# Matmuls on zeros ahead of the first inputs, and the last row's normalising factor by square root and reciprocal

## The chip, the core and the metric

The kernel runs on one NeuronCore of a Trainium2 chip. The core has five engines, each with its own instruction queue that is worked off in order: TensorE (PE, matrix products into PSUM), VectorE (DVE), ScalarE (ACT), GpSimd (POOL) and SyncE (SP, which here issues DMAs only). The metric is device time in microseconds; of three runs of the kernel before the median is 1186.96 us, with 1186.71 and 1188.21 at the ends.

## What is computed

The input is a sequence of 2048 positions with 576 channels. Four layers follow one another, each added to its input: Fourier mixing (A), a gated long convolution (B), A again, B again.

```python
def _A_ref(x, dft_seq_re, dft_seq_im, dft_hid_re, dft_hid_im):
    a = jnp.einsum("bsd,ed->bse", x, dft_hid_re)
    b = jnp.einsum("bsd,ed->bse", x, dft_hid_im)
    return jnp.einsum("ts,bse->bte", dft_seq_re, a) - jnp.einsum("ts,bse->bte", dft_seq_im, b)
...
x = A_x
x = x + _A_ref(_layernorm(x, axis=-1), A_dft_seq_re, A_dft_seq_im, A_dft_hid_re, A_dft_hid_im)
x = x + _B_ref(_layernorm(x, axis=-1), B_k, B_v, B_shift_k, B_ssm_k, B_ssm_D)
x = x + _A_ref(_layernorm(x, axis=-1), A_dft_seq_re, A_dft_seq_im, A_dft_hid_re, A_dft_hid_im)
x = x + _B_ref(_layernorm(x, axis=-1), B_k, B_v, B_shift_k, B_ssm_k, B_ssm_D)
```

`_layernorm` subtracts the mean of a row's 576 channels and divides by the square root of their variance plus 1e-5. The convolution branch of B depends on the weights and on B_k and B_v alone, so its result is computed once; in both B layers the normalised row is then multiplied by it, element by element.

## The kernel before

**Tiles.** The 2048 positions lie as 16 row blocks (J = 16) of 128 partitions by 576 channels. The sequence transform of layer A is done first: for each of four blocks of 512 output positions, for the cosine and for the sine matrix, the 16 row blocks are summed up in PSUM. One such pair of a row block and a 128x512 tile of the transform matrix is called a step here, and step k of the first sixteen uses row block Xk and matrix tile ck. [...] A step multiplies hi by hi, hi by lo and lo by hi for four groups of 128 channels (12 matmuls into the accumulators `acc4`, tiles `s`) and, for the last 64 channels, does two more (tile `rm`): 14 matmuls of 512 columns (lines 318 to 332).

**What feeds a step.** Row block Xk is loaded from HBM (line 683), its statistics are taken on DVE (lines 181 to 183: two `bn_stats`, one `bn_aggr`, the variance plus 1e-5), GpSimd raises that to the power -1/2 (line 184), DVE makes the bias (line 190) and ACT normalises the row (line 191). From row block 8 on (`ASTAT`) ACT takes the sums instead (lines 649 and 651, with lines 650, 652 and 675 on DVE and the power on GpSimd, line 653; line 676 normalises). Then ACT writes the hi part (line 195) and DVE the lo part (lines 197 and 198). Matrix tile ck is loaded to a raw buffer (lines 168 and 216); ACT writes its hi part and DVE its lo part (lines 98 and 99 for the tile `mats`). There are three buffers for split matrix tiles, so the hi part of c(k+3) has to wait until step k has been multiplied.

**Beside it.** In the first steps runs the branch that prepares the convolution: its inputs are loaded (lines 366, 374, 418), combined on DVE (lines 393 and 398, 128x1152 each), split (lines 98 and 99, tile `f1r`) and multiplied in groups of six matmuls of 288 columns (tile `bf`, line 448), which ACT copies out of PSUM (line 451) and stores (line 452).

**Order.** The code is traced by generators: `layer` yields after pieces of a step, and the driver behind line 746 runs pieces of the branch between them. A planner at compile time then lays out each engine's instructions from what it knows of dependencies and costs; `tc.issue_after` (lines 101 to 106, `behind`) ties an instruction behind another one on its engine. So an engine's order in the trace need not be the order of the code.

**The end.** The last row blocks go through `hidden` (lines 276 to 289: 27 matmuls for each half of a row, added on DVE at line 287) and `done1`, where `gated` takes the statistics of the row (`norm_stats`), forms (row - mean) times the branch (line 665) and then multiplies by the factor and adds the row (line 668). For the last row block, j = 15, line 668 is done in two halves, and each half is sent to HBM at once (line 739, the first half from ACT's queue, the second from SP's).

**What the change touches.** The small tile `flts` (line 156) with -1/2 in its first column (lines 157 and 174); one ACT copy into its second column, which makes the ACT load its function table early (line 175); `gated` (line 656); and the driver between lines 750 and 751, where the first row block's load has been issued and no other work has been traced.

Of the kernel before, what the change touches and what calls it, by code (L numbers as in the profile page):

```python
# [10 lines left out]
F32 = mybir.dt.float32  # L11
FR = mybir.dt.float32r
AF = mybir.ActivationFunctionType
OP = mybir.AluOpType

P = 128
# [3 lines left out]
J = S // P  # L20
TB = 4
NT = 512
HD = D // 2
NC = 4
REM = D - NC * P
EPS = 1e-5
ASTAT = 8
XLEAD = 3
EARLY = 6
ROWS = (0, 1, 2, 3, 4, 5, 6, 7, 8, 9)  # L30
K_FIRST = 4
# [34 lines left out]
def fnet_h3_kernel(ctx: ExitStack, tc: tile.TileContext, x, c_mat, w_re, w_im, k_pad, v, shift_k,  # L66
                   ssm_k, ssm_d, f1c, i2c, midc, out):
    nc = tc.nc
# [5 lines left out]
    def mm(ps, lhsT, rhs, first, last, more=False):  # L74
        return nc.tensor.matmul(ps, lhsT, rhs, start=first, stop=last, skip_group_check=more).ins  # L75
# [10 lines left out]
    acc4 = [psp.tile([P, NT], F32, tag=f"s{i}", name=f"s{i}") for i in range(4)]  # L86
# [25 lines left out]
    def flat(words, dt, name):  # L112
        return sb.tile([P, words], dt, tag=name, name=name)
# [15 lines left out]
    ring = {}  # L129

    def lay(t, at, *sizes):

        for name, words, n in sizes:
            ring.setdefault(name, Ring()).tiles.extend(t[:, at + i * words:at + (i + 1) * words] for i in range(n))
            at += n * words
        assert at <= t.shape[1], (at, t.shape, sizes)
        return at
# [9 lines left out]
    xs = mats[:, :X_END].rearrange("p (j n) -> p j n", j=J)  # L147
# [6 lines left out]
    um = []  # L154

    flts = flat(FLT, F32, "flts")
    mhalf = flts[:, :1]
    lay(flts, 8, ("stat", STAT, 4))
    lay(flts, RT_AT, ("rt", NT, 1))
    lay(mats, X_END, ("cs", WIDE, 3))  # L160
# [5 lines left out]
    def load_after(dst, src):  # L166
        with tc.issue_after(anchor[-1]):
            return nc.sync.dma_start(dst, src).ins
# [3 lines left out]
            nc.gpsimd.dma_start(dst, src)  # L172

    nc.vector.memset(mhalf, -0.5)
    nc.scalar.activation(flts[:, 1:2], mhalf, AF.Copy)

    def norm_stats(src):
        m = ring["stat"]()
        st, mv, ve, rs = m[:, :12].rearrange("p (a c) -> p a c", a=2), m[:, 12:14], m[:, 14:15], m[:, 15:16]
        for i in range(2):  # L180
            nc.vector.bn_stats(st[:, i, :], src[:, i * HD:(i + 1) * HD])
        nc.vector.bn_aggr(mv, st)
        nc.vector.tensor_scalar(ve, mv[:, 1:2], EPS, None, op0=OP.add)  # L183
        pows.append(nc.gpsimd.tensor_tensor(rs, ve, mhalf, OP.pow).ins)  # L184
        return mv, rs, m[:, 16:17]
# [27 lines left out]
    def load_c(step):  # L213
        g, tb, k = step
        raw = ring["craw"]()
        anchor.append(load_after(raw, c_mat[g, tb, k]) if anchor else nc.sync.dma_start(raw, c_mat[g, tb, k]).ins)
        c = ring["cs"]()
        t = c[:, :NT], c[:, NT:]
        with behind(*stored):
            halved[:] = split(t[0], t[1], raw)  # L220
        CT[step] = t
# [3 lines left out]
    def load_w():  # L225
        lay(flts, SC_AT + CRAW * NT + 4 * D, ("wl", D, 3))
        wg = region_a(FR, "w").rearrange("p (k n) -> p k n", k=9)
        for ch in (8, *range(8)):
            w = two(wg[:, ch])
            raw = ring["wl"]()  # L230
            if ch < 8:
                nc.sync.dma_start(raw, (w_re if ch < 4 else w_im)[(ch % 4) * P:(ch % 4 + 1) * P, :])
            else:
                nc.sync.dma_start(raw[:REM], w_re[NC * P:, :])
                nc.sync.dma_start(raw[REM:], w_im[NC * P:, :])
            for lo, hi, sg in ((0, P, 1 if ch < 4 else -1),) if ch < 8 else ((0, REM, 1), (REM, P, -1)):
                if sg > 0:
                    split(w[lo:hi, 0, :], w[lo:hi, 1, :], raw[lo:hi])
                else:
                    nc.scalar.activation(w[lo:hi, 0, :], raw[lo:hi], AF.Copy, scale=-1.0)  # L240
                    nc.vector.scalar_tensor_tensor(w[lo:hi, 1, :], raw[lo:hi], -1.0,  # L241
                                                   w[lo:hi, 0, :].bitcast(F32), op0=OP.mult,
                                                   op1=OP.subtract)
            W[ch] = w
            yield
        for ch in range(9):
            load_after(w_d[ch], wg[:, ch].bitcast(F32))
            yield
# [42 lines left out]
    def finish(pending, pieces):  # L291
        while pending and pieces:
            if not isinstance(pending[0], types.GeneratorType):
                pending[0] = hidden(*pending[0])
            if next(pending[0], 0) == 0:
                pending.pop(0)
            else:
                pieces -= 1

    def layer(get_x, xres, done, pending, blocks=TB):  # L300
        steps = [(g, tb, k) for tb in range(blocks) for g in range(2) for k in range(J)]
        for n, (g, tb, k) in enumerate(steps):
# [3 lines left out]
            if n + 2 < len(steps):  # L306
                load_c(steps[n + 2])
            for i in range(XLEAD + 1 if blocks == TB else 1):
                if n + i < J:
# [336 lines left out]
    def sums(src, junk):  # L646
        m = ring["stat"]()
        sm, sv, rs, nb = (m[:, i:i + 1] for i in range(4))
        nc.scalar.activation(junk, src, AF.Copy, accum_out=sm)
        nc.vector.tensor_scalar(sm, sm, -1.0 / D, None, op0=OP.mult)  # L650
        nc.scalar.activation(junk, src, AF.Square, bias=sm, accum_out=sv)
        nc.vector.tensor_scalar(sv, sv, 1.0 / D, EPS, op0=OP.mult, op1=OP.add)
        pows.append(nc.gpsimd.tensor_tensor(rs, sv, mhalf, OP.pow).ins)
        return sm, rs, nb

    def gated(xa, q, j, junk=None, last=None):
        load_after(q, yb_d[j])
        if junk is None:
            mv, rs, _ = norm_stats(xa)
            mean, op = mv[:, 0:1], OP.subtract  # L660
        else:
            mean, rs, _ = sums(xa, junk)
            op = OP.add
        yield
        nc.vector.scalar_tensor_tensor(q, xa, mean, q, op0=op, op1=OP.mult)
        for i in range(2 if last else 1):
            cs = slice(i * HD, (i + 1) * HD) if last else slice(None)
            nc.vector.scalar_tensor_tensor(q[:, cs], q[:, cs], rs, xa[:, cs], op0=OP.mult, op1=OP.add)
            if last:
                last(i, cs)  # L670

# [8 lines left out]
    def load_x(j):  # L680
        if j < J:
            XL[j] = ring["x"]()
            nc.sync.dma_start(XL[j], x[:, j, :])
# [7 lines left out]
    def get_x0(j):  # L691
        if X[j] is None:
            if j > 0:
                load_x(j + 2)
            stats0(j)
            if j > 0:
                with behind(*stored):
                    stats0(j + 1)
            src, ln = LN[j]
            with behind(*rounded[-1:]):  # L700
                next(ln, 0)
            X[j] = to_x(src, j)
# [4 lines left out]
    def make_x1(j):  # L707
        xa, q = ring["xa"](), ring["yb"]()
        load_after(xa, xa_d[j])
        for _ in gated(xa, q, j, ring["xj"]() if j % 2 and j >= EARLY else None):  # L710
            yield
        for _ in normed_x(q, xa, ring["xj"]()):
            to_store.append((xb_d[j], q))
            yield
        to_store.append((y_d[j // 2][:, j % 2, :], xa))
        X[j] = to_x(xa, j)
        ready.add(j)
# [3 lines left out]
    def advance(j=None):  # L721
        while to_store:
            load_after(*to_store.pop(0))
        with behind(*halved, *added, *evac):
            for row in list(making):
                if next(row, 0) == 0:
                    making.remove(row)
            if j is not None:
                making.append(make_x1(j))
                next(making[-1])  # L730
# [4 lines left out]
    def done1(j, xa):  # L735
        q = ring["yb"]()

        def store(i, cs):
            (nc.scalar if i == 0 else nc.sync).dma_start(out[:, j, cs], q[:, cs])

        for _ in gated(xa, q, j, last=store if j == J - 1 else None):
            pass
        if j < J - 1:
            nc.sync.dma_start(out[:, j, :], q)

    pending = []
    lay(flts, SC_AT, ("craw", NT, CRAW))
    br = branch()
    wl = load_w()
    load_x(0)  # L750
    next(br)
    get_x0(0)
    with tc.issue_after(biased[0]):
# [18 lines left out]
    for n, whole in layer(get_x0, lambda j: x[:, j, :], done0, pending):  # L772
# [30 lines left out]
        m = n - PREP  # L803
# [9 lines left out]
        if 0 <= m and n < HOLD:  # L813
            advance(m // 2 if m % 2 == 0 and m < 2 * EARLY else None)
    T, R, t7 = {}, {}, []
# [126 lines left out]
    cs, done = {}, []  # L942
# [68 lines left out]
    for n, whole in layer(get_x1, lambda j: xb_d[j], done1, pending, 1):  # L1011
# [4 lines left out]
        if n == 0:  # L1016
            for name, at in (("xa", 0), ("yb", 4 * D)):
# [3 lines left out]
                lay(gate, at, (name, D, 4))  # L1021
        advance(EARLY + ROWS.index(n) if n in ROWS else None)
        finish(pending, 1)
# [131 lines left out]
```

## Time and profile before

| what | value |
|---|---|
| median of three runs | 1186.96 us |
| the profiled execution's own time | 1186.46 us |
| its span, first to last instruction | 1184.5 us |
| time outside the span | 1.96 us |
| PE busy / weight loads busy | 1165.9 / 988.1 us |
| DVE / ACT / POOL busy | 868.8 / 650.6 / 75.0 us |

A row of the timeline gives the start of a group of equal instructions in us from the start of the span, how long the group lasts, the engine, the line of the kernel, the operation, what it writes and reads, the size and how many there are; in brackets stands the idle time of the engine before it and what ended that. An engine name with a q (SPq, ACTq) is the engine's own queue work, such as issuing a DMA. [...]

### The profile page before, as it was taken

Reading aid. Unit: us, or ns where it says so; the run is one execution under the profiler, and the core shown is the slowest. Engines: PE = TensorE matmul, PEld = TensorE weight load, DVE = VectorE, ACT = ScalarE, POOL = GpSimd, SP = SyncE. Lnnn points to the kernel's source line nnn. Section 1 sums busy time; section 2 is a strip of 40 time slices with the busy share of each in tenths; the row PEclk is TensorE's granted clock in tenths of the full one; section 3 lists DMA queues with packets and bytes.
Section 4 is the critical chain, followed back from the end, with each engine's and each line's share of the span. In section 5 each row is a group of like instructions: output and inputs, shape, how many; then the busy total and the mean of one; then the engine's idle time right before and its main releaser. Section 6 shows DMA issues by size and latency. Waiting matters only on the chain.

```text
span 1184.5 us, 18056 instructions
## 1 busy us (share of the span) xinstructions
PE 1165.9 (98%) x6184; PEld 988.1 (83%) x6184; DVE 868.8 (73%) x1562; ACT 650.6 (55%) x1279; POOL 75.0 (6%) x116
## 2 busy tenths in 40 slices
PE   7999999999999999999999999999999999999997
PEld 5776767888888888888888898888888888789997
DVE  7899983688877778787757765865776777775764
ACT  7865655578766668766645666534434445440200
POOL 2210000000000000001101111000000000001111
PEclk9999999999999999999999999999999999999999
DMA  9869898546666656648966776763762777894621
GB/s 341 297 194 313 268 294 267 177 148 182 213 198 201 198 169 201 193 139 250 267 191 218 244 251 232 246 239 88 251 240 72 244 271 255 270 318 157 212 84 41
DMA packets 147454, 255.65 MB, mean 216 GB/s; under 512 B 16161, under 2 KB 56353, under 8 KB 147362
## 3 DMA queue, kind: packets, MB, share of 16 engines
q1 hardware_dynamic: 111890, 210.17, 55.5%
q10 hardware_dynamic: 28560, 37.91, 9.1%
q0 software_dynamic: 6912, 6.43, 2.5%
q8 instruction: 48, 0.79, 0.3%
q14 instruction: 44, 0.36, 0.1%
HBM read 187.80 MB, written 66.65 MB: 215 GB/s over the span
## 4 chain that ended last, share of the span: by engine, by line
PE 77%; ACT 2%; DMA 1%; DVE 1%; issue 0%; ACTq 0%; POOLq 0%; DVEq 0%
PE s L75 43%; PE bk L75 30%; PE rm L75 4%; ACT flts L512 1%; ACT mid L512 1%; DMA t<-ud 1%; DMA flts<-in_c_mat 0%; ACT mats L98 0%; DVE mid L518 0%; DVE flts L532 0%; DVE flts L531 0%; DVE t L99 0%; ACT u L98 0%; POOLq L1151 0%; ACTq L548 0%
## 5 line engine op out<-in xcount | busy, mean ns | idle before, releaser
L75 PE MATMUL s<-mats 128*128 128x512 f32 x2088 | 542.3, 395 | 1.1 <-ACT mats L195 1.0
L75 PEld LDWEIGHTS s<-mats 128*128 128x128 f32 x2088 | 381.0, 188 | 82.2 <-issue 10.6
L99 DVE TENSOR_TENSOR mats<-flts,mats 128x512 fp32r<-128x512 f32 x206 | 140.7, 687 | 52.2 <-ACT mats L98 51.0
L98 ACT ACTIVATE mats<-flts 128x512 fp32r<-128x512 f32 x206 | 128.3, 627 | 82.8 <-PE bk L75 29.6
L75 PE MATMUL bk<-mid 128*128 128x288 f32 x704 | 126.4, 300 | 1.4 <-DVE flts L287 0.6
L75 PEld LDWEIGHTS bk<-mid 128*128 128x128 f32 x704 | 108.5, 188 | 22.0 <-ACT flts L512 5.0
L512 ACT ACTIVATE flts<-bk 128x288 f32<-128x288 f32 (+1 forms) x192 | 76.5, 405 | 90.2 <-PE bk L75 76.5
L75 PE MATMUL bk<-w,u 128*128 128x288 f32 x864 | 120.9, 295 | 0.4 <-DVE w L241 0.4
L75 PEld LDWEIGHTS bk<-w,u 128*128 128x128 f32 x864 | 117.5, 188 | 3.7 <-ACT flts L512 0.9
L518 DVE TENSOR_TENSOR mid<-flts,mid 128x576 fp32r<-128x576 f32 (+1 forms) x149 | 93.4, 627 | 19.0 <-ACT mid L512 16.3
L75 PE MATMUL rm<-mats 128*128 128x512 f32 x304 | 94.8, 391 | 0.2 <-ACT flts L512 0.2
L512 ACT ACTIVATE mid<-flts 128x576 fp32r<-128x576 f32 (+1 forms) x148 | 80.5, 576 | 9.6 <-DVE flts L533 5.1
L287 DVE TENSOR_TENSOR flts<-flts,bk 128x288 f32<-128x288 f32 x48 | 21.8, 453 | 66.8 <-PE bk L75 64.3
L75 PE MATMUL bk<-mats 128*128 128x288 f32 (+1 forms) x376 | 67.8, 317 | 0.0
L451 ACT ACTIVATE flts<-bf 128x384 f32<-128x384 f32 (+1 forms) x104 | 43.1, 463 | 44.9 <-PE bf L75 44.8
L75 PEld LDWEIGHTS rm<-mats 128*128 128x128 f32 x304 | 57.1, 188 | 12.8 <-ACT flts L512 0.6
L75 PE MATMUL s<-t,mats 128*128 128x512 f32 x264 | 65.4, 390 | 0.6 <-DVE t L99 0.3
L184 POOL TENSOR_TENSOR flts<-flts 128x1 f32<-128x1 f32 x35 | 28.7, 820 | 521.9 <-DVE flts L183 521.8
L75 PE MATMUL bk<-mats,t 128*128 128x288 f32 (+1 forms) x368 | 59.3, 303 | 0.0
L75 PEld LDWEIGHTS s<-t,mats 128*128 128x128 f32 x264 | 49.4, 188 | 11.7 <-DVE t L99 0.8
L512 ACT ACTIVATE flts<-flts 64x288 f32<-64x288 f32 x128 | 56.6, 442 | 4.5
L75 PEld LDWEIGHTS bk<-mats 128*128 128x128 f32 x376 | 55.6, 188 | 3.4
(146 smaller groups left out, 1495.3 us busy)
## 6 DMA issues: line engine op xcount, KB each, us to landing
flts<-in_c_mat SPq DMA_DIRECT2D x148, 256.0 KB, 3.4
ph<-in_c_mat SPq DMA_DIRECT2D x54, 512.0 KB, 4.3
flts<-in_c_mat SPq DMA_DIRECT2D x30, 512.0 KB, 5.1
flts<-td SPq DMA_DIRECT2D x53, 288.0 KB, 3.0
td<-flts ACTq DMA_DIRECT2D x36, 384.0 KB, 4.5
vd<-flts ACTq DMA_DIRECT2D x64, 144.0 KB, 2.5
flts<-vd SPq DMA_DIRECT2D x32, 288.0 KB, 4.0
ud<-ph ACTq DMA_DIRECT2D x12, 512.0 KB, 6.6
```

What stands on the lines that cost most here:

```text
L75: return nc.tensor.matmul(ps, lhsT, rhs, start=first, stop=last, skip_group_check=more).ins
L98: a = nc.scalar.activation(h, src, AF.Copy).ins
L99: return a, nc.vector.tensor_tensor(l, src, h.bitcast(F32), OP.subtract).ins
L184: pows.append(nc.gpsimd.tensor_tensor(rs, ve, mhalf, OP.pow).ins)
L287: added[:] = [nc.vector.tensor_tensor(r[:, cs], r[:, cs], ps[:, :HD], OP.add).ins]
L451: stored[:] = [nc.scalar.activation(so[:, i, :], ps[i], AF.Copy).ins]
L512: last_act.append(nc.scalar.activation(*args, **kw).ins)
L518: nc.vector.tensor_tensor(l, src, h.bitcast(F32), OP.subtract)
```

## The change

At the start, DVE writes zeros into the first 512 columns of the place where row block 15 will be put later, and TensorE multiplies these zeros by themselves 14 times, 128x128 by 128x512, into the accumulator `acc4[3]`. Nothing reads the product: the first real matmul into `acc4[3]` starts its sum anew.

For the last row block alone, `gated` leaves out the addition of 1e-5 on DVE and the power on GpSimd. ACT takes the square root of the variance plus 1e-5 (given as the bias, from a third column of `flts`), and DVE takes the reciprocal after line 665. The early ACT instruction that makes it load its table is a square root now instead of a copy. All other rows keep the power on GpSimd.

```diff
+WARM = 14
...
-    mhalf = flts[:, :1]
+    mhalf, eps = flts[:, :1], flts[:, 2:3]
...
     nc.vector.memset(mhalf, -0.5)
-    nc.scalar.activation(flts[:, 1:2], mhalf, AF.Copy)
+    nc.vector.memset(eps, EPS)
+    nc.scalar.activation(flts[:, 1:2], eps, AF.Sqrt)
...
     def gated(xa, q, j, junk=None, last=None):
         load_after(q, yb_d[j])
-        if junk is None:
+        if last:
+            m = ring["stat"]()
+            st, mean, var = m[:, :12].rearrange("p (a c) -> p a c", a=2), m[:, 12:13], m[:, 13:14]
+            for i in range(2):
+                nc.vector.bn_stats(st[:, i, :], xa[:, i * HD:(i + 1) * HD])
+            nc.vector.bn_aggr(m[:, 12:14], st)
+            rs, op = m[:, 14:15], OP.subtract
+            nc.scalar.activation(var, var, AF.Sqrt, bias=eps)
+        elif junk is None:
             mv, rs, _ = norm_stats(xa)
             mean, op = mv[:, 0:1], OP.subtract
...
         nc.vector.scalar_tensor_tensor(q, xa, mean, q, op0=op, op1=OP.mult)
+        if last:
+            nc.vector.reciprocal(rs, var)
         for i in range(2 if last else 1):
...
+    def warm():
+        t = xs[:, J - 1, :NT]
+        nc.vector.memset(t.bitcast(F32), 0.0)
+        for i in range(WARM):
+            mm(acc4[3], t[:, :P], t, i == 0, i == WARM - 1)
+
...
     load_x(0)
+    warm()
     next(br)
     get_x0(0)
```

More of the change, by code (lines that the diff above doesn't have):

```diff
@@ L665, in gated @@
         nc.vector.scalar_tensor_tensor(q, xa, mean, q, op0=op, op1=OP.mult)
+        if last:
+            nc.vector.reciprocal(rs, var)
         for i in range(2 if last else 1):
             cs = slice(i * HD, (i + 1) * HD) if last else slice(None)
-            nc.vector.scalar_tensor_tensor(q[:, cs], q[:, cs], rs, xa[:, cs], op0=OP.mult, op1=OP.add)
+            nc.vector.scalar_tensor_tensor(q[:, cs], q[:, cs], rs, xa[:, cs],
+                                           op0=OP.mult, op1=OP.add)
             if last:
```

## The prediction

> **What bounds the kernel now.** I read the page's busy times first, then PE's waits over the whole span, then the timeline of its two ends, where the change lies.
>
> ```profile
> PE 1165.9 (98%) x6184; PEld 988.1 (83%) x6184; DVE 868.8 (73%) x1562; ACT 650.6 (55%) x1279; POOL 75.0 (6%) x116
> ```
> ```profile
> PE bf L75 <- DVE f1r L99: 6.6, 1, 6.6
> PE s L75 <- ACT mats L195: 1.0, 2, 0.8
> ```
> PE is busy for 98% of the span. Of the 18.6 us in which it is not, 6.6 are the wait for the first inputs, and the next longest wait is 0.8 us. So what can be won lies in the wait at the start, in the rate just behind it, and after the last matmul.
>
> ```profile
> 6.61 1.09 PE L75 MATMUL bf<-f1r 64*128 64x288 f32 x6 [6.61 <-DVE f1r L99]
> 7.92 1.73 PE L75 MATMUL s<-mats 128*128 128x512 f32 x2 [0.22 <-ACT mats L195]
> 9.66 1.09 PE L75 MATMUL bf<-f1r 64*128 64x288 f32 x6
> 10.68 4.53 PE L75 MATMUL s<-mats 128*128 128x512 f32 x10
> 15.04 0.63 PE L75 MATMUL rm<-mats 128*128 128x512 f32 x2
> 15.51 2.88 PE L75 MATMUL s<-mats 128*128 128x512 f32 x12
> 18.23 0.62 PE L75 MATMUL rm<-mats 128*128 128x512 f32 x2
> 18.68 2.88 PE L75 MATMUL s<-mats 128*128 128x512 f32 x12
> ...
> 21.95 0.67 PE L75 MATMUL bf<-f1r 64*128 64x288 f32 x6
> 22.54 3.05 PE L75 MATMUL s<-mats 128*128 128x512 f32 x12
> ```
> Step 0 begins at 7.92 and step 1 at 15.51. Ten matmuls start between 10.68 and 15.04, 0.436 us each; in step 1 twelve start between 15.51 and 18.23, 0.227 each. TensorE thus runs at half its later rate until about 14.9, 8.3 us after its first matmul. At 0.227 the ten would take 2.3 us instead of 4.4. The product groups `bf` show the same: 1.09 us early, 0.67 later.
>
> **Part 1, the zeros.** They remove nothing; they add one DVE memset and 14 matmuls ahead of PE's first work.
>
> ```profile
> 0.81 0.06 DVE L174 MEMSET flts<- 128x1 f32 x1 [0.81 <-PEq L1147]
> 3.66 0.82 DVE L181 BATCH_NORM_STATS2 flts<-early 128x6 f32<-128x288 f32 x2 [2.79 <-DMA early<-in_x]
> ```
> A memset of 128x512 is not in the trace. The 128x1 one bounds it below (0.06 us), a DVE subtraction of that size (0.68, the row of line 198 below) above. It is one pass over one operand, so I take the upper end. Both small memsets and this one lie in DVE's 2.79 us of idling, so they cost nothing; behind them waits the first `bn_stats`, which would be late only if they lasted until 3.66. PE can then start at 1.0 to 1.7. At 0.427 to 0.436 the 14 matmuls take 6.0 to 6.1 us and end by 7.8 at the latest, against the 6.61 at which real work is ready. That delays the first `bf` group by up to 1.2 us, to 7.8 to 8.9. Behind it stands step 0's first matmul (7.92), and its second needs the lo part of c0, written at 8.12 to 8.79. The ACT copy of that group's result starts at 8.91 (below). So the delay costs 0.1 us or nothing, more so as the rate should have doubled by then: PE took 8.3 us with gaps from its first matmul until the doubling, and 8.3 us after 1.5 is 9.8, without gaps sooner.
>
> With the rate doubled before 9.66, the second `bf` group (held until 9.60 by the ACT copy of the first) lets step 0 go on at 9.66 + 0.59 = 10.25 (0.59 is 22.54 - 21.95). Its remaining 12 matmuls at 0.227, with 0.1 for the switch between shapes, end at 13.1. Before, the next step began at 15.51: **2.4 us**. What has to be ready next is X1:
>
> ```profile
> 8.12 0.67 DVE L99 TENSOR_TENSOR mats<-flts,mats 128x512 fp32r<-128x512 f32 x1
> 8.91 0.69 ACT L451 ACTIVATE flts<-bf 128x288 f32<-128x288 f32 x2
> 13.55 0.67 ACT L195 ACTIVATE mats<-early 128x576 fp32r<-128x576 f32 x1
> 15.09 0.68 DVE L198 TENSOR_TENSOR mats<-early,mats 128x512 fp32r<-128x512 f32 x1
> ```
> Its hi part is there at 14.22, its lo part at 15.77, and neither waited for PE. By the code the third matmul of a step needs lo: it could then start at 15.8 instead of 15.96, a gain of 0.16. The order on the chip is another:
>
> ```profile
> 56.28 1.19 PE L75 MATMUL s<-mats 128*128 128x512 f32 x4 [0.77 <-ACT mats L195]
> ```
> ```profile
> 56.72 0.68 DVE L198 TENSOR_TENSOR mats<-early,mats 128x512 fp32r<-128x512 f32 x1
> ```
> In step 12 four matmuls ran before the lo part was complete at 57.40. With four first, step 1's fifth starts at 15.8 instead of 16.42: 0.6. With all eight that need hi alone, only 14.22 binds: 15.51 - 14.27 = 1.24. I take **0.9**, between the two; the ends are 0.16 and 1.24.
>
> Will the feeding engines follow? Where PE's progress held ACT, they can:
>
> ```profile
> 15.48 0.63 ACT L98 ACTIVATE mats<-flts 128x512 fp32r<-128x512 f32 x1 [0.50 <-PE rm L75]
> 18.65 0.63 ACT L98 ACTIVATE mats<-flts 128x512 fp32r<-128x512 f32 x1 [0.64 <-PE rm L75]
> 22.65 0.71 ACT L451 ACTIVATE flts<-bf 128x288 f32<-128x288 f32 x2 [0.55 <-PE bf L75]
> 52.16 0.71 ACT L451 ACTIVATE flts<-bf 128x288 f32<-128x288 f32 x2 [1.73 <-PE bf L75]
> 55.56 0.67 ACT L195 ACTIVATE mats<-early 128x576 fp32r<-128x576 f32 x1
> ```
> ```profile
> 30.91 1.35 DVE L393 TENSOR_TENSOR f1f<-f1f 128x1152 f32<-128x1152 f32 x1
> ```
> ```profile
> 52.83 0.14 DVE L650 TENSOR_SCALAR flts<-flts 128x1 f32<-128x1 f32 x1
> ```
> ```profile
> f1f<-in_shift_k SPq DMA_DIRECT2D x1, 576.0 KB, 8.6
> ```
> PE's only long wait after the start, 0.77 us at 56.28, is for X12's hi part (line 195 at 55.56). A PE that comes 0.9 earlier would wait 0.9 longer there unless X12 moves too. ACT's part of that chain starts at 52.16, after 1.73 us of waiting for PE, so it moves with PE until it needs DVE's line 650 (done at 52.97, used at 53.28 by line 651): 0.3 of slack. DVE works nearly without a break from 30.91 on, and that instruction needs shift weights whose DMA was issued at 21.90 and took 8.6 us: there at 30.5. So DVE can come forward by 0.4 and X12 by 0.4 + 0.3 = **0.7 us**. This is the term: 0.7, with 0 (all of it swallowed there) and 1.24 as its ends. Behind 56.3, PE's waits sum to some 2 us with none above 0.6, so a shift passes on.
>
> [...]
>
> **Part 2, the last row.**
>
> ```profile
> 1177.80 0.21 DVE L182 BATCH_NORM_AGGREGATE flts<-flts 128x2 f32<-128x12 f32 x1
> 1178.04 0.15 DVE L183 TENSOR_SCALAR flts<-flts 128x1 f32<-128x1 f32 x1
> 1178.11 0.81 DVE L665 SCALAR_TENSOR_TENSOR ph<-ph,flts 128x576 f32<-128x576 f32 x1
> 1178.34 0.99 POOL L184 TENSOR_TENSOR flts<-flts 128x1 f32<-128x1 f32 x1 [6.17 <-DVE flts L183]
> 1179.36 0.94 DVE L668 SCALAR_TENSOR_TENSOR ph<-ph,flts 128x288 f32<-128x288 f32 x2 [0.44 <-POOL flts L184]
> ```
> Now line 668 waits for the power, 0.44 us after line 665 is done. Line 183 goes, so line 665 starts at 1178.04 and ends at 1178.85. The square root starts on an idle ACT near 1178.05; the trace has no 128x1 ACT instruction with a bias operand, but even 0.67 us, the price of 128x576 (line 195), would end it at 1178.72, under line 665. The reciprocal is new: like the 128x1 and 128x2 rows above 0.15 to 0.21. It starts up to 0.07 before line 665 ends (line 665 itself starts 0.08 before line 183 ends), so it ends at 1178.93 to 1179.06 and line 668 starts at 1178.95 to 1179.1. Against 1179.36 that is 0.26 to 0.41: **0.36 us**. The two stores behind keep their distance. Nothing else on ACT or POOL waits there.
>
> The early square root moves only the table's kind: ACT loads a table at the start either way.
>
> **Sum.** The profiled execution took 1186.46 us (span 1184.5 and 1.96 outside): 1186.46 - 0.7 - 0.36 = 1185.4. The median of the runs lies 0.50 above the profiled one, so for a median I expect 1186.96 - 1.06 = **1185.9 us**, its own range 1185.1 to 1186.7.
>
> **The rivals.** *Nothing at the start.* Either products of zeros don't count as work and the rate doubles at 14.9 as before, or the gain is swallowed whole at 56.28. Only the 0.36 remains: 1186.6. For it: DVE is packed from 30.91 on. Against it: ACT's 1.73 us of waiting for PE.
>
> *The whole of step 0 passes.* If the planner, which sees new work on PE, lays out DVE so that X1 is split earlier, all 2.4 us are kept: 1186.96 - 2.4 - 0.36 = 1184.2. For it: between 10 and 15 us DVE does statistics of later rows ahead of X1's lo part. Against it: X1's hi part itself is not there before 14.22, and the edit doesn't touch these lines.
>
> *The clock falls back*, the slower side. A faster step 0 leaves PE idle from 13.1 to 14.27, 1.2 us, where it was continuously fed.
>
> ```profile
> 1175.50:1178.50 3.00, 1.28 (x10) 1.04 (x8) 1.58 (x5) 0.00 (x0) 0.16 (x1) 1.00 0.00 0
> 1178.50:1179.00 0.50, 0.00 (x0) 0.00 (x0) 0.42 (x1) 0.00 (x0) 0.50 (x1) 0.90 0.00 0
> ```
> At the end PE's last work ends at 1176.78 (1.28 us into the first row's stretch) and the granted clock, 1.00 in that row and 0.90 in the next, halves at 1178.9: 2.1 us of idleness were enough, while 0.77 at 56.28 were not. The hole of 1.2 lies between. If it suffices, step 1 runs at half rate from 14.3 until PE has again been busy for as long as it took at the start: 5.2 us from the unbroken work at 9.66 to 14.9, or 8.3 from the first matmul. Half of that is lost, 2.6 to 4.2, against the 0.9 gained before it and the 0.36 at the end. On the median that is 1186.96 + 2.6 - 0.9 - 0.36 = 1188.3, up to 1189.9; the wait of 0.77 at 56.28 may take up that much again, 1187.5. It decides from the point where an idle hole of 1.2 us counts like one of 2.1.
>
> [...]
>
> *A table load at the end.* ACT_TABLE_LOAD takes 1.28 us at the start:
>
> ```profile
> 0.74 1.28 ACT L175 ACT_TABLE_LOAD   x1 [0.74 <-PEq L1147]
> ```
> If the square root needs another one at the end, it ends at 1178.05 + 1.28 + 0.3 = 1179.6, line 668 starts at 1179.8, 0.4 late instead of 0.36 early: 1186.96 - 0.7 + 0.4 = 1186.7. Against it: line 175 now asks for the square root first. [...]
>
> **How the numbers follow.** The forecast has 0.50, nothing at the start 0.15, the whole of step 0 0.17, the clock 0.13, the table 0.05. From 1184.0 to 1188.6 the range takes in the faster rival and most of the clock's. A measurement tells about 0.2%, 2.4 us, from no change: faster is below 1184.6, slower above 1189.3. Faster gets the second rival and the forecast's edge, 0.20; slower the clock's upper end and an unlucky layout, 0.10; the rest, 0.70, is no change.
>
> **What would show it.** Right: 14 matmuls from about 1.5 us; `bf` at 9.66 in some 0.67; step 0 done near 13.1 and a new wait of about 1.2 us before step 1; step 1 starting near 14.3 and step 12 near 55.6; on the last row no POOL instruction, and line 668 starting about 1.0 us after line 665 (1.25 before). Wrong: starts 0.43 us apart after 9.66, or again in step 1 (clock); step 12 at 56.3 (swallowed); step 1 at 13.1 (whole gain); a second table load; or an order of DVE or ACT that differs from the one quoted.

## The result and the profile after

The changed kernel takes **1183.85 us** in the median of ten runs (1183.03 to 1185.47), the kernel before 1186.86 (1185.51 to 1188.21) beside it: a ratio of 0.9975, 95% interval 0.9965 to 0.9984, so 3.0 us or 0.25% less. The forecast was 1185.9 with 1184.0 as the lower end of its range: the sign was right, the gain nearly three times as large as forecast, and the time just outside the range. The profiled execution took 1183.61 us, its span 1181.8 (1184.5 before).

In the changed kernel the lines stand 1 to 20 further down: 76 is the matmul, 99 and 100 the splits, 197 and 200 the hi part of a row block (the operand rounded) and its lo part (the rest), 395 and 400 the convolution, 651 to 655, 688 and 689 the sums. The page's first part, and PE's longest waits over the span:

```profile
PE 1167.8 (99%) x6198; PEld 989.1 (84%) x6198; DVE 868.6 (73%) x1564; ACT 650.8 (55%) x1280; POOL 75.5 (6%) x115
```
```profile
PE s L76 <- ACT mats L197: 2.4, 2, 1.4
PE s L76 <- DVE mats L761: 1.5, 1, 1.5
```
PE is idle for 14.0 of 1181.8 us (18.6 before). The wait of 6.6 for the first inputs has become one of 1.5 for the memset of line 761. The two waits for a hi part (line 197), 2.4 us together, are the most that is left. The start, in PE's timeline:

```profile
1.52 5.00 PE L76 MATMUL s<-mats 128*128 128x512 f32 x14 [1.52 <-DVE mats L761]
6.49 0.66 PE L76 MATMUL bf<-f1r 64*128 64x288 f32 x6
8.17 0.73 PE L76 MATMUL s<-mats 128*128 128x512 f32 x2 [1.02 <-ACT mats L197]
9.09 0.73 PE L76 MATMUL s<-mats 128*128 128x512 f32 x2 [0.18 <-DVE mats L100]
9.75 0.66 PE L76 MATMUL bf<-f1r 64*128 64x288 f32 x6
10.34 2.11 PE L76 MATMUL s<-mats 128*128 128x512 f32 x8
12.29 0.63 PE L76 MATMUL rm<-mats 128*128 128x512 f32 x2
14.30 3.03 PE L76 MATMUL s<-mats 128*128 128x512 f32 x12 [1.38 <-ACT mats L197]
17.17 0.61 PE L76 MATMUL rm<-mats 128*128 128x512 f32 x2
17.63 0.62 PE L76 MATMUL s<-mats 128*128 128x512 f32 x2
```
The last product of zeros ends at 6.52, just as the first `bf` group becomes ready (it starts at 6.49 and PE doesn't idle before it), and that group already takes 0.66 us, not 1.09. Step 0 is done at 12.9, PE then waits 1.38 us for X1's hi part, step 1 begins at 14.30 and step 2 at 17.63, 1.05 us sooner than before (18.68). Up to here things went as forecast. They part at step 12:

```profile
51.06 3.00 PE L76 MATMUL s<-mats 128*128 128x512 f32 x12
53.90 0.62 PE L76 MATMUL rm<-mats 128*128 128x512 f32 x2
54.36 1.72 PE L76 MATMUL s<-mats 128*128 128x512 f32 x6
```
Step 12 begins at 54.36, 1.92 us sooner (56.28 before, 55.6 forecast), and the wait of 0.77 that stood before it is gone. PE's timeline counts most of it out: 1.05 brought from step 2, and the 0.77, make 1.82. In all, PE needs 36.73 us from step 2 to step 12, and 37.60 before.

The last row, in the timeline of all engines:

```profile
1176.22 0.21 DVE L665 BATCH_NORM_AGGREGATE flts<-flts 128x2 f32<-128x12 f32 x1
1176.46 0.29 ACT L667 ACTIVATE flts<-flts 128x1 f32<-128x1 f32 x1 [50.46 <-DVE flts L665]
1176.46 0.82 DVE L675 SCALAR_TENSOR_TENSOR ph<-ph,flts 128x576 f32<-128x576 f32 x1
1177.19 0.16 DVE L677 RECIPROCAL flts<-flts 128x1 f32<-128x1 f32 x1
1177.39 0.95 DVE L680 SCALAR_TENSOR_TENSOR ph<-ph,flts 128x288 f32<-128x288 f32 x2
```
From the end of the aggregate to the last multiply there are 0.96 us, 1.35 before (1179.36 - 1178.01): 0.39 gained, 0.36 forecast. But from the start of that multiply to the end of the span there are 4.43 us here and 5.18 before. These 0.75 us are in no term of the forecast.

**Where step 12's gain comes from.** X12's hi part hangs on DVE's small line 650 (652 after): ACT's line 651 (653) uses its result and stands 2.3 us ahead of the hi part on ACT. DVE's timeline between 38 and 42 us, before:

```profile
38.25 0.68 DVE L99 TENSOR_TENSOR mats<-flts,mats 128x512 fp32r<-128x512 f32 x1
39.19 0.15 DVE L652 TENSOR_SCALAR flts<-flts 128x1 f32<-128x1 f32 x1 [0.27 <-ACT early L651]
40.01 0.16 DVE L675 TENSOR_TENSOR flts<-flts 128x1 f32<-128x1 f32 x1 [0.66 <-POOL flts L653]
40.71 0.15 DVE L652 TENSOR_SCALAR flts<-flts 128x1 f32<-128x1 f32 x1 [0.55 <-ACT early L651]
41.53 0.16 DVE L675 TENSOR_TENSOR flts<-flts 128x1 f32<-128x1 f32 x1 [0.66 <-POOL flts L653]
```
and after:

```profile
38.43 0.16 DVE L688 TENSOR_TENSOR flts<-flts 128x1 f32<-128x1 f32 x1 [0.60 <-POOL flts L655]
38.54 0.69 DVE L100 TENSOR_TENSOR mats<-flts,mats 128x512 fp32r<-128x512 f32 x1
39.15 0.22 DVE L199 TENSOR_TENSOR mats<-early,mats 128x64 fp32r<-128x64 f32 x1
39.28 0.68 DVE L200 TENSOR_TENSOR mats<-early,mats 128x512 fp32r<-128x512 f32 x1
39.89 1.35 DVE L400 TENSOR_TENSOR f1f<-f1f 128x1152 f32<-128x1152 f32 x1
41.16 0.14 DVE L654 TENSOR_SCALAR flts<-flts 128x1 f32<-128x1 f32 x1
```
These are not the same instructions at another time, but another order. Before, two chains of sums stood one behind the other on DVE, each handed to ACT and GpSimd and back, and DVE idled 2.1 us over them. After, a split, a row's lo part and a convolution add lie between. When the engines' instruction lists of the two kernels are compared without line and buffer numbers, some 55 of PE's instructions, 35 of ACT's and 55 of DVE's stand at another place, far more than the change adds. The planner laid out the first steps anew.

Rows of DVE's and ACT's timelines and of the windows' busy times give the sum. Of after:

```profile
30.47 1.35 DVE L395 TENSOR_TENSOR f1f<-f1f 128x1152 f32<-128x1152 f32 x1
```
```profile
50.97 0.15 DVE L652 TENSOR_SCALAR flts<-flts 128x1 f32<-128x1 f32 x1
```
```profile
51.15 0.78 ACT L653 ACTIVATE early<-early,flts 128x576 f32<-128x576 f32 x1 [1.25 <-DVE flts L652]
...
53.45 0.67 ACT L197 ACTIVATE mats<-early 128x576 fp32r<-128x576 f32 x1
...
54.78 0.39 ACT L453 ACTIVATE flts<-bf 128x288 f32<-128x288 f32 x1
```
```profile
30.47:51.12 20.65, 20.65 (x103) 15.76 (x101) 19.29 (x38) 17.04 (x38) 7.94 (x4) 1.00 0.95 342
```
and of before, from its first convolution multiply at 30.91 to the end of line 650 at 52.97 (the third figure behind the length is DVE's busy time):

```profile
30.91:52.97 22.06, 22.06 (x109) 16.97 (x108) 19.92 (x37) 18.26 (x42) 5.81 (x4) 1.00 0.87 313
```
The first multiply comes 0.44 us sooner. From it to the small instruction DVE needs 20.65 us instead of 22.06: 0.78 less idle time (1.36 against 2.14) and 0.63 less work put ahead of it. And ACT now waits for DVE, where it used it 0.31 late before (53.28 against 52.97; now 51.15 against 51.12, 0.28 less). Together 2.13 us, and X12's hi part moves by 55.56 - 53.45 = 2.11. ACT's order matters as much: before, two copies of a product group, which waited 1.73 us for PE, and the split of a matrix tile stood ahead of line 651 (52.16 to 53.28); after, the copies (line 453) come at 54.78, behind the hi part, which no longer waits for PE.

### The profile page after: what moved, and what is told of

Its sections match the earlier page's. It is cut to its first block, busy times and chain, and to the rows that moved or that the text cites. A ratio compares the mean times of both kernels' runs of the same rounds, so it can differ in the third digit from the quotient of the medians.

```text
span 1181.8 us, 18082 instructions
## 1 busy us (share of the span) xinstructions
PE 1167.8 (99%) x6198; PEld 989.1 (84%) x6198; DVE 868.6 (73%) x1564; ACT 650.8 (55%) x1280; POOL 75.5 (6%) x115
## 3 DMA queue, kind: packets, MB, share of 16 engines
q1 hardware_dynamic: 111890, 210.17, 55.6%
## 4 chain that ended last, share of the span: by engine, by line
PE 77%; ACT 2%; DVE 2%; DMA 1%; issue 1%; ACTq 0%; DVEq 0%
PE s L76 43%; PE bk L76 30%; PE rm L76 4%; ACT flts L514 1%; ACT mid L514 1%; DVE mid L520 0%; DMA flts<-td 0%; DMA flts<-in_c_mat 0%; ACT mats L99 0%; DVE flts L534 0%; DVE flts L533 0%; DVE flts L532 0%; DVE flts L535 0%; ACTq L550 0%; ACT u L99 0%
## 5 line engine op out<-in xcount | busy, mean ns | idle before, releaser
L76 PEld LDWEIGHTS bk<-mats 128*128 128x128 f32 x376 | 55.6, 188 | 3.4
```

## The experiments

Two questions were open. Is it the new order that gives the 2 us, or the early clock by itself, which a reader of the start alone would name? And is the 0.75 at the end the power's doing? The plan of the order is made at compile time, from what the planner thinks the work costs, so kernels can be built that have the early clock with the old order, and the new order with a later clock. The instruction lists of such kernels show how many zeros turn the order:

| matmuls of 512 zero columns | order of the engines' instructions, zeros left out |
|---|---|
| 0, 1, 2, 4, 6, 8, 10, 11 | that of before (but for the last row) |
| 12, 14, 16, 20, 28 | that of after |

No kernel of this table has an order between the two. Five memsets and one product of zeros also give that of after.

**The last row alone**, in the old order:

```diff
     load_x(0)
-    warm()
     next(br)
```


> The last row's square root and reciprocal without any matmul on zeros. Both theories (earlier clock, new order of the engines) say the same: the factor's path at the end is shorter by 0.39 us as in the changed kernel's trace (bn_aggr's end to line 668's start 0.96 instead of 1.35 us), so 1186.9 - 0.4 = 1186.5 us, no difference that can be told. If the end is worth more than that (the stores of the last row landed 0.8 us sooner in the changed kernel's trace), 1185.7.


Measured: 1186.98 us (ratio 0.9989, 0.9980 to 0.9997), with 0.96 us from aggregate to multiply and 4.41 from there to the end. Step 12 begins at 56.54, with the wait of 0.77 before it. So the last row gives about 1 us, and nothing comes from the start.

**Eleven zeros**, the most that leave the old order:

```diff
-WARM = 14
+WARM = 11
```


> The whole change with 11 matmuls on zeros instead of 14; with 11 the planner leaves every engine in the order of the kernel before. Theory clock: TensorE's rate doubles early just as well, step 0 ends near 13 us, and nearly all of the 3 us comes, 1184.0. Theory order: the early clock alone is worth what was forecast, 0.7 at step 12, and the rest of the 1.9 us won there came from the new order of ACT and DVE: 1185.8, with step 12 at about 55.6 instead of 54.4.


Measured: 1187.91 us (1.0001, 0.9992 to 1.0011). Windows of 3.41 us, in which the page's clock (third figure from the end) changes:

```profile
4.66:8.07 3.41, 1.76 (x11) 1.02 (x9) 1.28 (x5) 2.35 (x4) 1.20 (x2) 1.00 1.00 344
8.07:11.48 3.41, 2.00 (x6) 0.99 (x8) 3.11 (x8) 2.51 (x6) 0.00 (x0) 0.50 1.08 382
```
The clock doubles at 4.66 (the products of zeros start 0.43 us apart before it and 0.23 behind it), and at 8.07, with PE busy for 1.76 of the 3.41 us before, it falls back to half until 14.90. Step 12 begins at 57.04, later than before, and the last row's gain is used up. This is the third rival (the clock falls back), in a kernel with three zeros fewer. As a test of the early clock in the old order it is spoilt.

**The new order with a later clock.** Five memsets hold PE back, and the planner is given one product of zeros:

```diff
-        nc.vector.memset(t.bitcast(F32), 0.0)
-        for i in range(WARM):
-            mm(acc4[3], t[:, :P], t, i == 0, i == WARM - 1)
+        for i in range(5):
+            nc.vector.memset(t.bitcast(F32), 0.0)
+        mm(acc4[3], t[:, :P], t, True, True)
```


> One matmul on zeros, behind five memsets on DVE instead of one; the planner then gives every engine exactly the order of the changed kernel, but TensorE is not kept busy, so its rate should double as late as before (14 to 16 us). Theory clock: the order is worth nothing, 1186.5 (the last row's 0.4 alone). Theory order: the order by itself brings 1 us or more, 1185.3 or less.


Its instructions stand in exactly the order of after. Measured: 1185.20 us (0.9974, 0.9964 to 0.9985). The start in PE's timeline, and step 12:

```profile
4.83 0.80 PE L76 MATMUL s<-mats 128*128 128x512 f32 x1 [4.83 <-DVE mats L762]
7.23 1.09 PE L76 MATMUL bf<-f1r 64*128 64x288 f32 x6 [1.60 <-DVE f1r L100]
...
54.77 1.75 PE L76 MATMUL s<-mats 128*128 128x512 f32 x6
```
Real work starts 0.7 us later than in the changed kernel and at half the rate (1.09 for a `bf` group), the clock doubles at 12.44 instead of 4.80, and still step 12 begins at 54.77 without a wait: 1.51 sooner than before, where the last row alone stood at 56.54. But this is not the new order at the clock of before, which doubled at 14.95: step 2 begins at 18.07 here, 0.61 sooner than before, and 0.90 of the 1.51 are won between step 2 and step 12.

**The change again**, on the same chip as these three, as their yardstick: the kernel is that of the change.


> The changed kernel once more on the same chip, as the mark for the other three: 1183.9 by both theories, 3.0 us under the kernel before.


Measured: 1185.20 us (0.9979, 0.9970 to 0.9988); step 12 at 54.47. The kernel with the later clock has the same median. In the traces a clock that doubles at 6.67 (here) instead of 12.44 is worth 0.3 us at step 12; the medians, with intervals of about 1 us to either side, show nothing of it.

**The early clock in the old order, with the zeros later**, so that no idle time comes between them and the real work:

```diff
-        nc.vector.memset(t.bitcast(F32), 0.0)
-        for i in range(WARM):
-            mm(acc4[3], t[:, :P], t, i == 0, i == WARM - 1)
+        for i in range(3):
+            nc.vector.memset(t.bitcast(F32), 0.0)
+        for i in range(8):
+            mm(acc4[3], t[:, :P], t, i == 0, i == 8 - 1)
```


> Eight matmuls on zeros behind three memsets, so that they run from about 2.8 to 6.3 us, right up to the first real work; the planner leaves every engine in the order of the kernel before. The clock should double between 6.3 and 9.7 us and stay doubled. Theory order (the gain at the start is the new order's, the clock is worth little by itself): 1186 to 1187 here against 1187.0 for the last row's change alone, so at most 0.9 us from the clock, as forecast for the old order. Theory clock: 1185.2 as the whole change.


Measured: 1186.79 us (0.9993, 0.9984 to 1.0002). In the profiled execution the clock doubled at 7.40 and fell back from 10.81 to 14.22:

```profile
7.40:10.81 3.41, 1.92 (x13) 0.90 (x11) 3.27 (x9) 2.43 (x5) 0.00 (x0) 1.00 1.04 364
```
```profile
56.04 1.91 PE L76 MATMUL s<-mats 128*128 128x512 f32 x6 [0.78 <-ACT mats L197]
```
PE won 0.3 us up to step 1 (15.21 against 15.51) and 0.24 up to step 12, where it waits 0.78 as before. Four of its eleven runs have a mean granted clock of 0.999, which leaves no room for such a fall (half of 3.41 us is 0.0014 of the time, and the halved clock at the end took another 0.0006 in this trace). They took 1186.29 to 1186.93 us, about 1.0 us below before, where the last row alone lay 0.9 below on its chip. So no gain of the early clock shows without the new order. Four runs are too few to exclude the 0.7 us forecast, and PE was not the forecast 0.9 ahead in the trace, so what a PE that far ahead would meet in the old order stays untested.

**From step 2 to step 12.** The traces of all these kernels separate what is won at the start from what is won behind it (all in us; the clock doubles where its record at full rate starts):

| kernel | order | clock doubles | step 2 | step 12 | between |
|---|---|---|---|---|---|
| before | old | 14.95 | 18.68 | 56.28 | 37.60 |
| last row alone | old | 14.60 | 18.94 | 56.54 | 37.60 |
| eleven zeros | old | 4.66, back from 8.07 to 14.90 | 19.44 | 57.04 | 37.60 |
| eight zeros, later | old | 7.40, back from 10.81 to 14.22 | 18.40 | 56.04 | 37.63 |
| five memsets, one product | new | 12.44 | 18.07 | 54.77 | 36.70 |
| the change again | new | 6.67 | 17.74 | 54.47 | 36.73 |
| the change | new | 4.80 | 17.63 | 54.36 | 36.73 |

In the old order step 12 follows step 2 by 37.60 to 37.63 us, whether PE came 0.28 us sooner or 0.76 later than before; the wait of 0.77 or 0.78 moves along, as ACT's copies ahead of X12 wait for PE. In the new order it follows by 36.70 to 36.73. So the new order is worth 0.9 us behind step 2, whatever the clock, and the lead at step 2 reaches step 12 in full. Of the 1.05 us of lead in the changed kernel, the kernel with the later clock has 0.61. How the 1.05 divides between clock and order is not shown.

**The old power beside the new factor.** This kernel computes the old addition and power of the last row as well, and nobody reads them:

```diff
             rs, op = m[:, 14:15], OP.subtract
+            nc.vector.tensor_scalar(m[:, 15:16], var, EPS, None, op0=OP.add)
+            nc.gpsimd.tensor_tensor(m[:, 16:17], m[:, 15:16], mhalf, OP.pow)
             nc.scalar.activation(var, var, AF.Sqrt, bias=eps)
```


> The changed kernel with the last row's old addition on DVE and power on GpSimd done beside the new path; their result is not read. Theory GpSimd tail (the last 0.8 us of the 1.2 that the last row brings comes from the end of the program, which waits for GpSimd to come to rest after its power): line 680's start to the end of the span goes back from 4.4 to 5.2 us, and the time is 0.8 to 0.9 above the changed kernel. Rival (the stores landed sooner by chance): no difference but 0.07 us on DVE.


Measured: 1185.80 us (0.9982, 0.9973 to 0.9991); 5.37 us from the last multiply to the end, against 4.43. **The zeros with the old last row** (the lines of the last row as before, the zeros kept) ran beside it:


> The 14 matmuls on zeros without the last row's change; the order of the engines is that of the changed kernel. Theory order with GpSimd tail: 1.2 us above the changed kernel, 1.8 below the kernel before. If the last row is worth the forecast 0.36 alone: 0.4 above the changed kernel.


Measured: 1185.62 us (0.9979, 0.9969 to 0.9988), 5.18 us from the last multiply to the end. In the traces both give the old tail, whoever uses the power's result. In the times, with no changed kernel on that chip, the two could not be told from each other or from the change.

**Root and reciprocal for the other rows too**: in the sums that ACT takes from row block 8 on, the round through GpSimd goes.

```diff
-        nc.vector.tensor_scalar(sv, sv, 1.0 / D, EPS, op0=OP.mult, op1=OP.add)
-        pows.append(nc.gpsimd.tensor_tensor(rs, sv, mhalf, OP.pow).ins)
+        nc.scalar.activation(sv, sv, AF.Sqrt, bias=eps, scale=1.0 / D)
+        nc.vector.reciprocal(rs, sv)
```


> The changed kernel with the same square root and reciprocal also where ACT takes a row's sums (lines 649 to 653 of the kernel before): each row loses two hops between DVE and GpSimd, some 1.3 us of latency, and ACT gets a 128x1 instruction of 0.3 us more. The order of the engines changes again. If the waits of DVE for GpSimd (0.66 each) are what holds X9 to X15, step 12 comes up to 1 us sooner and the time is 0.5 to 1 us less; if a new order decides by itself, it can go either way by 1 to 2 us.


Measured: 1186.16 us (0.9985, 0.9976 to 0.9994), not better than the change. Step 12 begins at 54.48, so the powers there were not what held it back; the planner's order is yet another one (36.94 us from step 2 to step 12).

**Four kernels once more, side by side on one chip**, to size both parts in the time itself and not in single traces: the change, the change with the old power beside it, the zeros alone, and the last row alone.


> The changed kernel again, beside the three that follow, on one chip. Theory (the layout of the instructions gives some 1.6 to 2 us, the last row 1.17 us in the traces: 0.39 from the shorter chain and 0.78 because the end of the program no longer waits for GpSimd): 0.9973 to 0.9979 of before, the fastest of the four.

> The changed kernel, with the old addition and the old power of GpSimd on the last row computed beside the new factor and read by nobody. Theory: the time from the start of the last multiply to the end of the span goes from 4.43 to 5.37 us again, and the median of the runs is about 0.9 us above that of the changed kernel. Rival (the longer end lies inside what the program spends at its end anyway, so that it shows in the trace and not in the time): the same median as the changed kernel, within 0.3 us.

> The zeros with the old last row. Theory: 1.2 us above the changed kernel (0.9982 to 0.9988 of before). Rival (the last row is worth what was forecast, 0.36): 0.4 us above it.

> The new last row without zeros, in the old layout. Theory: 1.2 us below before (0.9990), some 1.6 us above the changed kernel. Rival (what the zeros change at the start is not carried to the end): the same as the changed kernel within 0.5 us.

| kernel | median us | ratio to before (95%) | step 12 | last multiply to end of span |
|---|---|---|---|---|
| before | 1187.69 | | 56.28 (first trace) | 5.18 (first trace) |
| the change | 1184.41 | 0.9974 (0.9964 to 0.9985) | 54.46 | 4.45 |
| old power beside | 1185.69 | 0.9982 (0.9973 to 0.9990) | 54.38 | 5.37 |
| zeros alone | 1186.03 | 0.9984 (0.9975 to 0.9992) | 54.34 | 5.18 |
| last row alone | 1186.47 | 0.9990 (0.9981 to 0.9998) | 56.26 | 4.41 |

The zeros give 1.66 us against before and 2.06 on top of the last row; the last row gives 1.22 alone and 1.62 on top of the zeros. The intervals are about 1 us wide to either side, but all four differences lie nearer to the theory (1.6 to 2 for the order, 1.2 for the last row) than to the rivals (none for the start, 0.4 for the last row). Between the medians, a power that nobody reads costs 1.28 us, with intervals that overlap; the traces show 0.92 of it behind the start of the last multiply (5.37 against 4.45). What it held up is seen in GpSimd's end-of-program instructions, in a view of the line that issues them (ns: shortest, median and longest; first and last start in us). Before:

```profile
L1151 POOLq EVENT_SEMAPHORE  x4: 17/17/17, 1183.4 to 1184.4; - x4
L1151 POOLq DRAIN  x3: 45/242/5019, 1178.3 to 1184.3; - x3
```
after, and with the old power beside:

```profile
L1171 POOLq EVENT_SEMAPHORE  x4: 17/17/17, 1180.6 to 1181.7; - x4
L1171 POOLq DRAIN  x3: 93/192/5022, 1169.6 to 1181.4; - x3
```
```profile
L1173 POOLq EVENT_SEMAPHORE  x4: 17/17/17, 1182.8 to 1183.7; - x4
L1173 POOLq DRAIN  x3: 45/93/5092, 1177.7 to 1183.6; - x3
```
In these three traces GpSimd's longest drain starts together with its last power (1178.34, 1169.59 and 1177.70) and lasts 5.02 to 5.09 us. Before, it began at 1178.3 and ended at 1183.33, and GpSimd's first semaphore of the end came at 1183.4; with the old power beside, drain and semaphore met at 1182.8. SyncE's first drain came sooner before:

```profile
L1151 SPq DRAIN  x3: 7/7/7, 1182.5 to 1183.6; - x3
```
so the end stood still for about 0.8 us, by an estimate from 1182.5 and 1183.33. After, the last power belongs to the row block before, the drain runs from 1169.6 to 1174.6 under PE's work, and GpSimd's first semaphore comes at 1180.6, with SyncE's first drain (1180.6). Before, the timeline shows 0.99 us of the power, and the end waited for the 5.02 of the drain. Whether another instruction of GpSimd would leave as long a drain was not tried.

## Why the prediction failed

**What held.** The zeros cost nothing, not even in the second trace of the change, where the clock doubled only at 6.67 and the first `bf` group began at 7.31: step 1 began at 14.41 there. The clock was doubled before 9.66 (the second `bf` group at 9.75 in 0.66 us); step 0 was done at 12.9 (13.1 forecast), the new wait was 1.38 us (1.2), step 1 began at 14.30 (14.3), and the gain at step 2 was 1.05 (0.9 forecast, between its bounds of 0.16 and 1.24). On the last row the multiply starts 0.39 us sooner after the aggregate (0.36), and there is one table load, 1.28 us at the start. The memset took 0.48 us, within its bounds of 0.06 and 0.68.

**The step that failed** is the term "X12 by 0.4 + 0.3 = 0.7 us". Its two summands came, 0.44 at the first convolution multiply and 0.28 of slack on ACT. What is missing is 1.41 us between them: the step took "DVE works nearly without a break from 30.91 on" as a fixed sequence that can only shift. But 2.14 of the 22.06 us were idle, and the planner, given more work for PE at the start, filled part of that, put less ahead of the small instruction that X12 needs, and moved the copies that wait for PE behind X12. So X12 came 2.11 us sooner and not 0.7. The 1.05 us that PE brought were not cut to 0.7 but passed in full, and the wait of 0.77 that the forecast left in place went as well. The second part is the new order's: all traces that have it need 36.67 to 36.74 us from step 2 to step 12, all of the old order 37.60 to 37.63. The first part, the lead at step 2, is the one that the forecast derived from the early clock; the runs don't show how much of it the clock alone would bring.

The limit given for the 0.4 was wrong as well, although its size came true. The multiply was said to need the shift weights of the DMA issued at 21.90, there at 30.5. After, the same transfer is issued at 22.50 and takes 9.0 us:

```profile
f1f<-in_shift_k SPq DMA_DIRECT2D x1, 576.0 KB, 9.0
```
It lands at 31.5, and the multiply starts at 30.47: it does not need that transfer.

**The second step that failed** is the sentence "The two stores behind keep their distance. Nothing else on ACT or POOL waits there." The stores do; the program's end does not hang on them alone. GpSimd's drain behind the removed power set it, and the 0.36 was mis-sized by the missing 0.75. In the traces the last row is worth 0.39 + 0.75 = 1.14 us, in the side-by-side runs 1.2 to 1.6.

A slip in the sum is small beside these: from the bounds that the prediction gives, the lower end of the forecast's own range would be 1186.96 - 1.24 - 0.41 = 1185.3, not 1185.1.

**The rivals.** "The whole of step 0 passes" named the right cause, a planner that lays out DVE otherwise, and at 1184.2 nearly the right time, but at the wrong place. X1's hi part starts at 13.58 (13.55 before), so 1.2 of the 2.4 us are lost there as the forecast said, and the time is won again at step 12. That "the edit doesn't touch these lines" was the fault in the reasoning: the order of lines that an edit doesn't touch changed all the same. At a chance of 0.17 its time was taken as the edge of the range, with nothing left below it. "Nothing at the start" and "A table load at the end" are refuted by step 12 and by the single load. "The clock falls back" did not happen here, but with three zeros fewer it did.

**What adds up.** In the traces, 1.92 us at step 12 and 1.14 at the end make 3.06; the medians fell by 3.0. That the two agree so closely is partly luck. Between 60 us and the end single executions drift apart by up to 3 us: the last matmul starts 1.58 us sooner in the trace of after than in that of before, although it was 2.1 us ahead at the 250th after the zeros. The second trace of the last row alone stands where before does at step 12 (56.26 against 56.28) and starts its last matmul 2.97 later; a window at half the clock (215.71 to 219.12) accounts for 1.7 of that, by an estimate of half its length. What fraction of the 2 us arrives can therefore not be read from a pair of traces; the medians say 1.7 to 2.1.

**Open.** Neither a kernel with the old order whose clock stays up in every run was obtained, nor one with the new order whose clock doubles as late as before. What the early clock alone is worth rests on one kernel and four of its runs, and its share of the 1.05 us before step 2 stays open.

## What to carry to other kernels

Where a planner orders the instructions, an added piece of work is also an input to the plan: compare the order of each engine before crediting a gain to the mechanism that was meant, and build the new order without the mechanism and the mechanism without the new order. Then look whether each kernel really is what it was built to be, and compare the time between two fixed points of the bottleneck engine: here the 37.6 and 36.7 us from step 2 to step 12 tell the order's gain from a lead brought along. A stretch that looked packed, its engine 90% busy (19.92 of 22.06 us), gave back 0.78 of its 2.14 us of idle time when the order changed, so its slack belongs in the bounds. And the end of this program waited for GpSimd's drain, 5.02 us from the start of a power of 0.99: look at what the last instruction on each side engine leaves behind it.

## What the runs showed of the hardware

**GpSimd's drain** lasted 5.02 us from the start of its last power in the traces of before, of after and of the zeros alone, and 5.09 with the old power beside; the power's own row shows 0.99, and 1.05 with the old power beside. Before, the multiply that used the power started 1.05 us into the drain (1179.36), so the result was there long before the drain's end.

**Matmul records** overlap: in step 1 of before, twelve take 389 ns each in the mean and start 0.227 us apart. Rates here are therefore read from starts.

**The clock.** In the changed kernel the products of zeros start 0.43 us apart up to 4.67 and 0.23 apart from 4.97 on, with the record at full rate starting at 4.80. In the three traces whose table rows have zeros from 1.52 on, the clock doubled 3.1 to 5.2 us later: at 4.66 (eleven zeros), 4.80 (the change) and 6.67 (the change again). Where it fell and came back, it stayed down for 3.41 us (10.81 to 14.22 and 215.61 to 219.02 with the eight zeros) or 6.83 (8.07 to 14.90 with the eleven).

It fell after windows in which PE was far from idle: busy 1.76 of 3.41 (eleven zeros), 1.92 (eight zeros) and 1.29 before the end of the kernel before. It stayed up with 2.03 of 3.41 in the changed kernel's own hole before step 1:

```profile
11.62:15.03 3.41, 2.03 (x9) 1.38 (x8) 3.06 (x13) 2.99 (x6) 3.02 (x5) 1.00 1.05 369
```
These are windows of single executions; what makes the clock fall is not shown. It also fell in mid-kernel in some executions: in both traces of the last row alone (from 215.98 and 215.71; their mean granted clock is 0.997), and in the one profiled of the eight zeros, where a window 1.59 us busy was followed by one at half rate:

```profile
212.20:215.61 3.41, 1.59 (x10) 1.15 (x9) 1.86 (x3) 2.03 (x4) 0.00 (x0) 1.00 0.42 103
215.61:219.02 3.41, 3.36 (x12) 2.44 (x11) 2.48 (x4) 0.31 (x1) 0.00 (x0) 0.50 0.47 134
```
Such a fall costs half of 3.41, some 1.7 us by estimate: more than most parts of this change.
